# A fused attention and mixing kernel: other token tiles in the two rotation groups of the first batch

## The chip, the cores and the metric

One Trainium2 chip, one core. The metric is the device time of one execution in microseconds; lower is better. Three runs of the kernel before gave 989.75, 991.41 and 989.65 us, median 989.75.

## The reference, cut to what matters

Four batches, 8 heads, 576 tokens, 64 numbers per head (512 per token), in f32.

```
scores = q @ k^T / 8;  keep the 32 largest of each row;  attn = softmax;  x = attn @ v
theta  = x @ w_theta
zr, zi = x * cos(theta), x * sin(theta)
y      = w_tok_r @ zr + w_tok_i @ zi          # over the 576 tokens
u      = x + y;   x2 = u + relu(u @ w_ch)
h      = relu(x2 @ w_in);  u2, v2 = halves of h
out    = (u2 * (w_spatial @ layernorm(v2) + b_spatial)) @ w_out
```

The lines that matter here are the second to the fourth: the rotation (theta, cosine, sine and the two products) and the token mixing.

## The kernel before, in words

**Attention.** Work goes by tiles of 128 query rows; a batch has 4 pairs of heads with 9 tiles each, so 36 tiles, and two tiles make a group. For a group PE makes the scores (L449), ACT copies them to x (L453), and DVE finds the 32nd largest score of every row in a *round*: pairwise maxima and minima (L468, L469), maxima of eight (L472, L478), removals (L481), and the coefficients cf (L491). ACT then makes a sign and an exponential (L500, L501), POOL multiplies them (L89, written as sg), PE transposes (L511), ACT copies to ptb (L512), and PE multiplies by the values (L522 to L536). The result is normalised into xn. There are 72 rounds, on 144 tiles. x has three buffers, so fresh scores wait until POOL has done with those three groups earlier.

**The later layers** of batch b are run as a generator beside the attention of batch b + 1. Every product there is made of three matmuls on high and low parts (`mm3`, L572 to L574), since both operands are split in two. All instructions that a wrapper issues at raised priority carry L588. Parts of the generator of interest:

- `rotate(order)` works on the given token tiles (0 to 3 have 128 tokens, 4 the last 64). For every tile `theta` makes 12 matmuls, a rounding on ACT and DVE, and an absolute value on ACT. Then come the sines (cosines by a shifted bias) on ACT, for all tiles of the group together, in two halves of 256 columns. Then, for every quarter of 128 columns, DVE makes x * cos and x * sin, POOL copies the high part of the cosine product (zah) and DVE takes the low part (zal). In a second loop ACT copies the high part of the sine product (zbh) and POOL makes the low part (zbl). While they are angles, the same buffers appear in the trace as zbl and zbh; the sine product is written over xn.
- The last 64 tokens stand twice on the partitions, so that one sine with a bias of half a turn in one half gives both products; they form term 8.
- `middle(b)` begins with token mixing: 8 sums (4 blocks of 128 columns, 2 halves of 288 tokens) in PSUM, of 9 terms each: terms 0 to 3 are the cosine products of tiles 0 to 3, 4 to 7 the sine products, 8 the last tokens. A sum is added to F on DVE. Its PSUM tile, ps_m, has three buffers, shared with `theta`.

Batch 0 splits the rotation in two groups: `rotate((0, 1, 2))` is started when tile 36 is reached, before the last tiles of the batch are normalised, and `rotate((4, 3))` comes with the block of batch 0. The second group keeps its angles in two extra buffers (angle) and in r8. Token mixing of batch 0 takes the terms in another order than the other batches:

```python
terms = range(9) if b else (0, 1, 2, 4, 5, 6, 3, 7, 8)
```

so its first six terms need the first group alone. The other batches rotate all five tiles at once, in the order 0, 1, 4, 2, 3.

**What sets the order.** The generators yield costs, and `advance` lets them go on while the attention has given them credit. That and the priorities give the order of writing; a scheduler then lays down one list of instructions for every engine before the run. The split of the later weights into high and low parts (w_raw, w_f: L163 to L170, L211, L89, and SP's transfers) runs beside batch 0's attention and until round 26. The loads of the parts (L284) reuse the buffers of weights that are done with; `rotate` says so for w_theta when its group holds tile 4.

Of the kernel before, what the change touches and what calls it, by code (L numbers as in the profile page):

```python
# [10 lines left out]
F32 = mybir.dt.float32  # L11
F32R = mybir.dt.float32r
I32 = mybir.dt.int32
AF = mybir.ActivationFunctionType
OP = mybir.AluOpType
# [3 lines left out]
TURN = 6.283185  # L19
# [5 lines left out]
def sparse_attention_then_moe_kernel(  # L25
# [23 lines left out]
    NP = H // 2  # L49
# [19 lines left out]
    big = ctx.enter_context(tc.tile_pool(name="big", bufs=1))  # L69
# [37 lines left out]
    quarter, upright = constant(0.0, "quarter"), constant(math.pi / 2, "upright")  # L107
# [228 lines left out]
    def run(exact):  # L336
# [216 lines left out]

        XN = {}

        def normalise(b, j, lo, hi):
            if lo == 0:
                XN[b, j] = big.tile([128, 5, 2, D], F32, name="xn", bufs=6)
            xn = XN[b, j]
            i = slice(lo, hi)  # L560
            rs = tmp.tile([128, 5, 2], F32, name="rs")
            dve.tensor_scalar(rs[:, i], xr[:, i, :, D], 1e-9, None, op0=OP.add)
            dve.reciprocal(rs[:, i], rs[:, i])
            pool.tensor_tensor(xn[:, i], xr[:, i, :, 0:D], rs[:, i, :, None].to_broadcast([128, hi - lo, 2, D]),
                               op=OP.mult)
            if hi == 5:
                pool.tensor_tensor(xn[64:128, 4], xr[0:64, 4, :, 0:D],
                                   rs[0:64, 4, :, None].to_broadcast([64, 2, D]), op=OP.mult)


        def mm3(out, ah, al, bh, bl, first, last):
            pe.matmul(out, ah, bh, start=first, stop=False)  # L572
            pe.matmul(out, ah, bl, start=False, stop=False)  # L573
            pe.matmul(out, al, bh, start=False, stop=last)  # L574
# [82 lines left out]
        class Front:  # L657
# [59 lines left out]
            def rotate(self, order):  # L717

                ks = slice(min(order), min(max(order) + 1, 4))

                if order[0] == 0:
                    angles = zpair("b", F32)
                    rs, rc = (z[:, 0:2048].rearrange("p (k d) -> p k d", k=4)[:, ks] for z in angles)
                    r8 = angles[0][:, 2048:2560]
                else:
                    rs, rc = (big.tile([128, 1, 512], F32, name="angle", tag="xn", bufs=6) for _ in range(2))
                    r8 = t512()
                if self.b:
                    for i in order:
                        self.by_token(i, 0)  # L730
                    yield 2200
                for i in order:
                    if self.b == 0:
                        self.by_token(i, 0 if i == 4 else 3)
                    k = i - ks.start
                    ab = self.theta(i, *((r8, r8) if i == 4 else (rs[:, k], rc[:, k])))
                    yield 2600
                if 4 in order:
                    W.done(self.b, "th")

                with tc.issue_after(ab):
                    for d in (slice(0, 256), slice(256, 512)):
                        sin = uact.activation(rc[:, :, d], rc[:, :, d], AF.Sin, scale=-TURN, bias=upright)
                        uact.activation(rs[:, :, d], rs[:, :, d], AF.Sin, scale=-TURN)
                        if d.start == 0 and 4 in order:
                            with tc.issue_after(sin.ins):
                                uact.activation(r8, r8, AF.Sin, scale=-TURN, bias=quarter)
                zah, zal = self.za
                xs = [x_of(self.b, c) for c in range(4)]
                cols = [slice(c * 128, (c + 1) * 128) for c in range(4)]  # L750
                for x, d in zip(xs, cols):
                    udve.tensor_tensor(rc[:, :, d], x[:, ks], rc[:, :, d], op=OP.mult)
                    udve.tensor_tensor(x[:, ks], x[:, ks], rs[:, :, d], op=OP.mult)
                    if 4 in order:
                        udve.tensor_tensor(x[:, 4], x[:, 4], r8[:, d], op=OP.mult)
                    copy_pool(zah[:, ks, d], rc[:, :, d])
                    udve.tensor_tensor(zal[:, ks, d], rc[:, :, d], f32(zah[:, ks, d]), op=OP.subtract)
                    yield 1000
                if order[0] == 0:
                    self.zb = [z.rearrange("p (k d) -> p k d", k=5) for z in zpair("b")]  # L760
                zbh, zbl = self.zb
                ks = slice(ks.start, max(order) + 1)
                for i, (x, d) in enumerate(zip(xs, cols)):
                    copy_act(zbh[:, ks, d], x[:, ks])
                    self.turns[1 - i % 2].tensor_tensor(zbl[:, ks, d], x[:, ks], f32(zbh[:, ks, d]), op=OP.subtract)
                    yield 1000

        FR = {}

        def urgent(work):  # L770
            while True:
                with tc.high_priority(offset=FRONT):
                    c = next(work, None)
                if c is None:
                    return
                yield c
# [10 lines left out]
        def front(b):  # L787

            if b:
                FR[b] = Front(b)  # L790
                yield from FR[b].rotate((0, 1, 4, 2, 3))
            else:
                yield from urgent(FR[b].rotate((4, 3)))

        halves = [slice(0, HALF), slice(HALF, S)]

        def middle(b):
# [8 lines left out]
            for c in range(4):  # L806
                d = slice(c * 128, (c + 1) * 128)
                for m in halves:
                    p = mps([128, HALF])

                    terms = range(9) if b else (0, 1, 2, 4, 5, 6, 3, 7, 8)
                    for i, k in enumerate(terms):
                        mm3(p, *FR[b].z(k, d), th[k][:, m], tl[k][:, m], i == 0, i == 8)
                        if i == 5:
                            yield 1850
                    udve.tensor_tensor(F[:, c, m], p, F[:, c, m], op=OP.add)
                    lag.step(lambda c=c, m=m: ew.split(F[:, c, m], uh[:, c, m], ul[:, c, m]))
                    yield 1500
# [150 lines left out]
        def add_work(w):  # L969
            nonlocal work  # L970
            work = w if work is None else chain([work, w])
# [18 lines left out]
        def step(n):  # L990

            if n == RING:
                W.start()
            if n in EARLY:
                with tc.issue_after(FIRST[-1]):
                    early(EARLY.index(n))
            if n == PER:
                add_work(urgent(FR[0].rotate((0, 1, 2))))
            if n >= PER and (n - 4) % PER == 0:
                add_work(block(n // PER - 1))  # L1000
            if n < N:
                prepare(n)
# [90 lines left out]
```

## Time and profile before

| | |
|---|---|
| median of 3 runs | 989.75 us (989.65 to 991.41) |
| profiled execution | 992.02 us |
| its span, first to last instruction | 990.2 us |
| mean granted TensorE clock | 0.901 |
| PE, DVE, ACT, POOL busy | 867.8, 823.0, 638.0, 598.7 us |

The profile shows one execution. PE is TensorE's matmuls, DVE VectorE, ACT ScalarE, POOL GpSimd; SP issues the DMAs. A line of code can be that of a helper, so groups are told apart by the tiles: `out<-in`. Consecutive instructions of one engine overlap a little at their ends, so busy times of single rows add up to slightly more than the stretch that they fill.

### The profile page before, as it was taken

To read this page: it belongs to the slowest core of one execution; us is meant where nothing else is said; L and a number is where in the kernel's file an instruction comes from. 1 tells how busy PE (TensorE), PEld (TensorE's weight loads), DVE (VectorE), ACT (ScalarE), POOL (GpSimd) and SP (SyncE) were. 2 spreads that over 40 slices of the span, in tenths; PEclk is the share of its full clock that TensorE was granted. 3 is DMA by queue.
4 is the path that set the end of the run, shared out by engine and by line. 5 is a ranking of instruction groups with operands and counts; after the bars stand their busy time and mean duration, and the time that the engine had idled before them with its cause. 6 is when DMAs were issued, how large, how long until landed. Compare 5 with 4: busy or idle time off the path is not lost.

```text
span 990.2 us, 18081 instructions
## 1 busy us (share of the span) xinstructions
PE 867.8 (88%) x5802; PEld 797.5 (81%) x5802; DVE 823.0 (83%) x2710; ACT 638.0 (64%) x1319; POOL 598.7 (60%) x753
## 2 busy tenths in 40 slices
PE   4657686678779799989999999999989999999997
PEld 2546575667669798888889998898889998889987
DVE  6999999999998897889999998999998981363552
ACT  5566676779858566877776777777966775350121
POOL 2798876686956755594767666676584564421030
PEclk9955556679779699999999999899999999999999
DMA  7797665545817633744362753552743554441221
GB/s 218 215 305 227 215 210 179 145 145 186 261 60 199 230 95 106 229 143 126 110 206 60 229 160 78 218 129 95 205 160 91 201 188 166 191 168 62 104 85 52
DMA packets 79395, 159.78 MB, mean 161 GB/s; under 512 B 36143, under 2 KB 40239, under 8 KB 71866
## 3 DMA queue, kind: packets, MB, share of 16 engines
q1 hardware_dynamic: 79290, 158.53, 50.5%
q8 instruction: 48, 0.79, 0.3%
q14 instruction: 57, 0.47, 0.2%
HBM read 108.63 MB, written 23.32 MB: 133 GB/s over the span
## 4 chain that ended last, share of the span: by engine, by line
PE 43%; DVE 26%; ACT 10%; DMA 9%; POOL 6%; issue 4%; SPq 2%; ACTq 0%; POOLq 0%; DVEq 0%
PE ps_m L574 9%; PE ps_m L572 9%; PE ps_m L573 9%; PE ps_v L533 7%; DVE mm L469 4%; PE ps_s L449 4%; PE ps_t L511 4%; DVE mm L481 4%; DVE mx L478 4%; DVE z L472 2%; DVE mm L468 2%; DMA raw<-in_q_dram 2%; DMA q<-hi 2%; ACT sg L500 1%; POOL sg L89 1%
## 5 line engine op out<-in xcount | busy, mean ns | idle before, releaser
L89 POOL TENSOR_TENSOR sg<-x,sg 128x288 f32<-128x288 f32 x288 | 238.5, 857 | 141.0 <-ACT x L501 94.2
L511 PE MATMUL ps_t<-ident,sg 128*128 128x128 f32 x648 | 140.9, 314 | 60.7 <-POOL sg L89 37.5
L533 PE MATMUL ps_v<-vc,ptb 128*128 128x65 f32 (+1 forms) x1280 | 183.5, 281 | 4.7 <-ACT ptb L512 4.7
L533 PEld LDWEIGHTS ps_v<-vc,ptb 128*128 128x128 f32 (+1 forms) x1280 | 174.7, 206 | 13.6 <-ACT ptb L512 6.7
L511 PEld LDWEIGHTS ps_t<-ident,sg 128*128 128x128 f32 x648 | 97.8, 171 | 77.6 <-POOL sg L89 51.2
L500 ACT ACTIVATE sg<-x,cf 128x576 f32<-128x576 f32 x144 | 103.8, 768 | 44.2 <-DVE cf L491 43.3
L478 DVE MAX8 mx<-mm 128x8 f32<-128x160 f32 x432 | 118.8, 312 | 0.0
L453 ACT ACTIVATE x<-ps_s 128x576 f32<-128x576 f32 x144 | 92.6, 643 | 35.9 <-PE ps_s L449 32.3
L512 ACT ACTIVATE ptb<-ps_t 128x640 f32<-128x640 f32 (+1 forms) x144 | 92.7, 644 | 29.8 <-PE ps_t L511 28.2
L501 ACT ACTIVATE x<-x,cf 128x576 f32<-128x576 f32 x144 | 107.9, 767 | 0.1
L449 PE MATMUL ps_s<-k,q 128*128 128x288 f32 x256 | 91.3, 368 | 16.2 <-DVE q L369 8.6
L572 PE MATMUL ps_m<-w_t,zah 128*128 128x288 f32 (+2 forms) x272 | 98.9, 364 | 6.6 <-DVE F L588 4.8
L574 PE MATMUL ps_m<-w_t,zal 128*128 128x288 f32 (+2 forms) x272 | 97.5, 360 | 0.6 <-POOL zal L89 0.5
L573 PE MATMUL ps_m<-w_t,zah 128*128 128x288 f32 (+2 forms) x272 | 96.7, 356 | 0.0
L472 DVE MAX8 z<-mm 128x8 f32<-128x312 f32 (+1 forms) x288 | 89.6, 372 | 2.0
L572 PE MATMUL ps_m<-w_t,zbh 128*128 128x288 f32 x288 | 85.7, 302 | 2.3 <-DMA w_t<-d_sph 1.0
L481 DVE MATCH_REPLACE8 mm<-mx,mm 128x160 f32<-128x160 f32 x288 | 86.8, 308 | 0.0
L573 PE MATMUL ps_m<-w_t,zbh 128*128 128x288 f32 x288 | 86.2, 303 | 0.0
L574 PE MATMUL ps_m<-w_t,zbl 128*128 128x288 f32 x288 | 84.9, 302 | 1.2 <-POOL zbl L89 1.2
L449 PE MATMUL ps_s<-kl,q 128*128 128x288 f32 x256 | 82.9, 334 | 0.0
L468 DVE TENSOR_TENSOR mm<-x 128x576 f32<-128x576 f32 x72 | 67.7, 941 | 17.5 <-ACT x L453 16.4
L89 POOL TENSOR_TENSOR raw<-raw,hi 128x288 fp32r<-128x288 f32 x60 | 56.2, 956 | 40.2 <-ACT hi L393 40.0
(174 smaller groups left out, 2438.9 us busy)
## 6 DMA issues: line engine op xcount, KB each, us to landing
k<-hi SPq DMA_DIRECT2D x60, 144.0 KB, 2.5
kl<-raw SPq DMA_DIRECT2D x60, 144.0 KB, 2.6
vc<-in_v_dram SPq DMA_DIRECT2D x48, 128.0 KB, 2.9
w_t<-d_trh SPq DMA_DIRECT2D x4, 1152.0 KB
w_t<-d_trl SPq DMA_DIRECT2D x4, 1152.0 KB
out_dram<-t SPq DMA_DIRECT2D x32, 144.0 KB, 2.5
raw<-in_q_dram SPq DMA_DIRECT2D x15, 288.0 KB, 3.0
q<-hi SPq DMA_DIRECT2D x30, 144.0 KB, 3.3
```

The lines of the kernel that those rows point to most:

```text
L89: nc.gpsimd.tensor_tensor(out[:, lo:hi], a[:, lo:hi], b[:, lo:hi], op=op)
L449: pe.matmul(o, q, k[:, m], start=a == 0, stop=a == len(terms) - 1)
L472: dve.max(out=z[:, i, QUARTER + 8 * k:QUARTER + 8 * k + 8], in_=mm[:, i, losers])
L478: last = dve.max(out=top[i], in_=src[i])
L481: dve.match_replace(out=mr[i], in_to_replace=top[i], in_values=src[i], imm_value=NEG)
L500: act.activation(sg, x, AF.Sign, bias=cf[:, 2:3])
L501: act.activation(x, x, AF.Exp, bias=cf[:, 0:1], scale=0.125)
L511: pe.transpose(pt[:, c, :], x[:, lo:lo + 128], ident)
L533: pe.matmul(o, pt[:, c, q], chunks[:, c, slot], start=alone and c == 0, stop=not alone and i == 1 and c == 3)
L572: pe.matmul(out, ah, bh, start=first, stop=False)
L573: pe.matmul(out, ah, bl, start=False, stop=False)
L574: pe.matmul(out, al, bh, start=False, stop=last)
```

## The change

Batch 0's first group gets tile 3, and the second keeps the last tokens alone. Since tile 3 of the last head pair may not have been normalised when the first group is started, the generator yields until it is (`WHOLE`). The last tokens' sine is issued by itself; the second group needs no angle buffers, no cosine and no low parts of it. Within each quarter the last tokens' product comes ahead of the others. Token mixing takes its terms in order in every batch, and the pause inside a sum is behind the fifth term instead of the sixth.

```diff
+        WHOLE = set()
...
             if hi == 5:
+                if j == NP - 1:
+                    WHOLE.add(b)
...
                 else:
-                    rs, rc = (big.tile([128, 1, 512], F32, name="angle", tag="xn", bufs=6) for _ in range(2))
                     r8 = t512()
...
                 for i in order:
+                    while i > 2 and self.b not in WHOLE:
+                        yield 600
...
                 with tc.issue_after(ab):
-                    for d in (slice(0, 256), slice(256, 512)):
+                    if order == (4,):
+                        uact.activation(r8, r8, AF.Sin, scale=-TURN, bias=quarter)
+                    for d in (slice(0, 256), slice(256, 512)) if order[0] == 0 else ():
...
                 for x, d in zip(xs, cols):
+                    if 4 in order:
+                        udve.tensor_tensor(x[:, 4], x[:, 4], r8[:, d], op=OP.mult)
+                    if order == (4,):
+                        continue
                     udve.tensor_tensor(rc[:, :, d], x[:, ks], rc[:, :, d], op=OP.mult)
                     udve.tensor_tensor(x[:, ks], x[:, ks], rs[:, :, d], op=OP.mult)
-                    if 4 in order:
-                        udve.tensor_tensor(x[:, 4], x[:, 4], r8[:, d], op=OP.mult)
...
-                yield from urgent(FR[b].rotate((4, 3)))
+                yield from urgent(FR[b].rotate((4,)))
...
-                    terms = range(9) if b else (0, 1, 2, 4, 5, 6, 3, 7, 8)
-                    for i, k in enumerate(terms):
-                        mm3(p, *FR[b].z(k, d), th[k][:, m], tl[k][:, m], i == 0, i == 8)
-                        if i == 5:
+                    for k in range(9):
+                        mm3(p, *FR[b].z(k, d), th[k][:, m], tl[k][:, m], k == 0, k == 8)
+                        if k == 4:
                             yield 1850
...
-                add_work(urgent(FR[0].rotate((0, 1, 2))))
+                add_work(urgent(FR[0].rotate((0, 1, 2, 3))))
```

The lists of instructions show what moves. DVE in the kernel before, from the start of round 22 (L588 are the rotation's instructions; zbl and zbh hold the angles, xn the attention output):

```order
L468 TENSOR_TENSOR mm<-x 128x2x288
L469 TENSOR_TENSOR mm<-x 128x2x288
L485 TENSOR_TENSOR flags<-z,mx 128x4
L588 TENSOR_TENSOR zbl<-xn,zbl 128x3x128 x4
L468 TENSOR_TENSOR z<-mm 128x2x144
L588 TENSOR_TENSOR xn<-xn,zbh 128x384 x4
L469 TENSOR_TENSOR mm<-mm 128x2x144
L588 TENSOR_TENSOR zal<-zbl,zah 128x3x128
L491 SCALAR_TENSOR_TENSOR cf<-cf,mx 128x2
L588 TENSOR_TENSOR zal<-zbl,zah 128x3x128
L588 COPY F<-ps_m 128x128
L588 TENSOR_TENSOR zal<-zbl,zah 128x3x128 x2
```

DVE in the changed kernel, from the start of round 23 (its L592 is the line that was L588); round 22 holds no product of the rotation there:

```order
L468 TENSOR_TENSOR mm<-x 128x2x288
L469 TENSOR_TENSOR mm<-x 128x2x288
L468 TENSOR_TENSOR z<-mm 128x2x144
L592 TENSOR_TENSOR zbl<-xn,zbl 128x4x128 x2
L469 TENSOR_TENSOR mm<-mm 128x2x144
L592 TENSOR_TENSOR zbl<-xn,zbl 128x4x128 x2
L592 TENSOR_TENSOR xn<-xn,zbh 128x512 x2
L472 MAX z<-mm 128x8 x4
L592 TENSOR_TENSOR xn<-xn,zbh 128x512
L592 TENSOR_TENSOR zal<-zbl,zah 128x4x128
L491 SCALAR_TENSOR_TENSOR cf<-cf,mx 128x2
L592 TENSOR_TENSOR xn<-xn,zbh 128x512
```

The rotation of tiles 0 to 3 stands one round later and in wider instructions, and the coefficients cf of round 23 stand behind eight of them.

SP's DMA issues in the kernel before, around the loads of w_tok_i's parts (d_tih, d_til); sp is w_spatial, w_f the buffers of the conversion:

```order
L199 DMA w_f<-in_moe_w_spatial_dram 128x576
L284 DMA w_t<-d_tih 128x2304
L409 DMA kl_2663<-raw 64x576 x2
L224 DMA d_sph<-w_f 128x576
L409 DMA kl_2664<-raw 64x576
L225 DMA d_spl<-w_f 128x576
L284 DMA w_t<-d_til 128x2304
```

and in the changed kernel:

```order
L225 DMA d_spl<-w_f 128x576
L409 DMA kl_2653<-raw 64x576
L408 DMA k_2651<-hi 64x576
L409 DMA kl_2653<-raw 64x576
L199 DMA w_f<-in_moe_w_spatial_dram 64x576
L224 DMA d_sph<-w_f 128x576
L199 DMA w_f<-in_moe_b_spatial_dram 1x576
L387 DMA raw<-in_q_dram 128x576
L225 DMA d_spl<-w_f 128x576
L284 DMA w_t<-d_tih 128x2304
L284 DMA w_t<-d_til 128x2304
```

Both loads have moved behind one more part of w_spatial and now stand next to each other.

## Rows read from the trace of the kernel before

**Rows 1.** The span in 40 slices, busy tenths of PE and DVE (page).

```profile
PE   4657686678779799989999999999989999999997
DVE  6999999999998897889999998999998981363552
```

**Rows 2.** Windows at rounds 22 to 25: busy us, instructions; clock, DMA share, GB/s.

```profile
246.30:266.60 20.30, 16.54 (x76) 13.87 (x76) 20.27 (x47) 16.68 (x32) 18.50 (x24) 0.72 0.77 242
266.60:282.20 15.60, 12.80 (x96) 11.82 (x95) 15.57 (x48) 13.26 (x26) 13.40 (x19) 1.00 0.51 163
282.20:299.50 17.30, 11.82 (x71) 11.59 (x70) 14.72 (x42) 8.29 (x18) 8.24 (x11) 0.70 0.19 59
299.50:314.80 15.30, 15.30 (x115) 13.95 (x114) 12.70 (x41) 11.50 (x22) 8.54 (x10) 1.00 0.79 217
```

**Rows 3.** DVE's groups by shape, 236 to 300 us: busy us, mean ns | idle before.

```profile
L588 DVE TENSOR_TENSOR xn<-xn,zbh 128x384 f32<-128x384 f32 x4 | 3.8, 1001 | 0.0
...
L588 DVE TENSOR_TENSOR zbl<-xn,zbl 128x384 f32<-128x384 f32 x4 | 3.3, 894 | 0.0
L588 DVE TENSOR_TENSOR zal<-zbl,zah 128x384 fp32r<-128x384 f32 x4 | 3.0, 762 | 0.0
L588 DVE TENSOR_TENSOR zal<-angle,zah 128x128 fp32r<-128x128 f32 x4 | 2.8, 768 | 0.0
...
L588 DVE TENSOR_TENSOR angle<-xn,angle 128x128 f32<-128x128 f32 x4 | 1.6, 456 | 0.0
...
L588 DVE TENSOR_TENSOR xn<-xn,angle 128x128 f32<-128x128 f32 x4 | 1.1, 326 | 0.0
...
L588 DVE SCALAR_TENSOR_TENSOR zbh<-t,ps_m 128x512 f32<-128x512 f32 x1 | 0.7, 650 | 0.0
```

**Rows 4.** DVE in order of time: start us, duration us, [idle before, releaser].

```profile
269.24 0.75 DVE L491 SCALAR_TENSOR_TENSOR cf<-cf,mx 128x2 f32<-128x2 f32 x1
...
282.18 2.93 DVE L468 TENSOR_TENSOR mm<-x 128x576 f32<-128x576 f32 x1
...
299.03 0.46 DVE L588 TENSOR_TENSOR F<-ps_m,F 128x288 f32<-128x288 f32 x1 [2.51 <-PE ps_m L574]
...
305.64 0.96 DVE L163 TENSOR_SCALAR w_f<-w_raw 128x512 int32<-128x512 int32 x1 [2.54 <-POOL sg L89]
...
324.55 1.42 DVE L468 TENSOR_TENSOR mm<-x 128x576 f32<-128x576 f32 x1
...
338.66 1.06 DVE L468 TENSOR_TENSOR mm<-x 128x576 f32<-128x576 f32 x1 [3.48 <-ACT x L453]
```

**Rows 5.** ACT in order of time, rounds 23 and 24.

```profile
267.15 1.28 ACT L588 ACT_TABLE_LOAD   x1
...
286.48 1.44 ACT L500 ACTIVATE sg<-x,cf 128x576 f32<-128x576 f32 x2 [3.86 <-DVE cf L491]
```

**Rows 6.** SP in order of time: the loads of w_tok_i's two parts.

```profile
254.12 0.33 SPq L284 DMA_DIRECT2D w_t<-d_tih  x1
...
262.43 0.33 SPq L284 DMA_DIRECT2D w_t<-d_til  x1
```

**Rows 7.** PE in order of time: token mixing (ps_m) and scores (ps_s) of rounds 22 to 27.

```profile
259.47 0.58 PE L572 MATMUL ps_m<-w_t,zah 128*128 128x288 f32 x1 [3.50 <-DVE F L588]
...
264.41 0.42 PE L574 MATMUL ps_m<-w_t,zal 128*128 128x288 f32 x1
...
266.01 0.51 PE L572 MATMUL ps_m<-w_t,zbh 128*128 128x288 f32 x2
...
266.50 0.29 PE L573 MATMUL ps_m<-w_t,zah 128*128 128x288 f32 x1
...
288.56 1.11 PE L511 MATMUL ps_t<-ident,sg 128*128 128x128 f32 x4 [5.48 <-ACT ptb L512]
...
295.21 0.39 PE L449 MATMUL ps_s<-k,q 128*128 128x288 f32 x1
...
324.15 0.29 PE L574 MATMUL ps_m<-w_t,zbl 128*128 128x288 f32 x1
```

## The prediction

> **What bounds the kernel now.** I read the slices of the span first. From the second slice DVE stands at 8 or 9 tenths, once at 7, up to slice 33, and at 1 to 6 behind it, while PE, at 4 to 8 in the first twelve, goes on at 9 almost to the end [rows 1]. So there are two regimes: up to the last of the 72 top-k rounds DVE sets the pace, and behind it PE works off the last batch alone. A microsecond that DVE saves before the last round moves the rest of the program forward, as long as PE and the buffers follow.
>
> I count a round from the first pairwise maximum on fresh scores (L468 with x as its input) to the next one. Batch 0's rotation lies in rounds 22 and 23, its token mixing in rounds 22 to 27. Next come the windows cut at these rounds [rows 2]: in round 22 (20.3 us) DVE is busy 20.27, in round 23 (15.6 us) 15.57, and PE has 16.54 and 12.80 there. In round 24 (17.3 us) DVE has 14.72 and PE 11.82: both wait. In round 25 PE is full.
>
> The order of instructions is laid down before the run, and between the two kernels it differs only in this stretch: from round 42 on each of the four compute engines and SP has the same list in both, row for row, to the end of the first run. What the change is worth is decided between rounds 21 and 41 and kept afterwards.
>
> **Part 1, DVE: 24 instructions become 12.** The first group's cosine product, sine product and cosine low part are three times four instructions of 128x384 [rows 3]: 3.3 + 3.8 + 3.0 = 10.1 us. The second group's are three times four of 128x128: 1.6 + 1.1 + 2.8 = 5.5 us. Together 15.6 us on a full DVE. Twelve of 128x512 replace them, all in round 23; the four products of the last tokens stay.
>
> No row has this operation at 512 columns. Lower end: a DVE instruction of 128x512 that reads one operand from PSUM has a mean of 0.65 us [rows 3], so 12 x 0.65 = 7.8. Upper end: the 384-column forms cost 10.1 / 12 = 0.84 each, and in proportion 512 columns would cost 1.12, so 13.4. I take the line through the two groups: 5.5 / 12 = 0.46 for 128 columns and 0.84 for 384 give 0.19 per 128 more, so 1.03 for 512, and 12 x 1.03 = 12.4. These are the nearest rows, because POOL works beside both kernels' rotation: in round 22 it is busy 18.50 of 20.3 us [rows 2]. **Gain 15.6 - 12.4 = 3.2 us**, between 2.2 and 7.8.
>
> **Part 2, the fourth sum of token mixing.** In round 24 DVE takes four sums from PSUM, and before the fourth it sits idle 2.51 us, until 299.03, for PE [rows 4]. Round 25 stands behind it in DVE's queue. In the new list that fourth addition stands in round 25, behind its pairwise instructions, so round 25 no longer waits for it. **Gain 2.5 us**; 0 if PE is as late for the third sum, which still stands in round 24.
>
> **What I cost at nothing.** The five theta products keep their number; tile 3's comes before that of the last tokens instead of after. ACT has nine sine instructions now and five then, with the same columns, and two table loads for sine and two back either way, 1.28 us each [rows 5]; ACT was busy 16.68 of 20.3 us in round 22 [rows 2], and that slack covers it; without it the first product would wait for the sines. POOL's high copies go from eight to four with the same columns; its sine low parts stay twelve, eight of 256 columns and four of 128. The moved pause inside a sum (behind the fifth term instead of the sixth) and the terms in order leave the 216 matmuls of the token mixing as they were.
>
> SP's queue is one that work is moved past. The loads of w_tok_i's two parts were issued at 254.12 and 262.43 [rows 6]; the first was used at 266.01 [rows 7], so it took at most 11.9 us. Now both stand behind a part of w_spatial that POOL has to finish first. I put both at the later of the two times, so they are there by 274 at the latest. Their first user comes behind the first sums' 24 cosine matmuls, at 272 or so (next part): at most 2 us of PE's time, which the margin there covers. Without it PE would be late by as much as the loads are.
>
> **Part 3, PE starts later.** The first token-mixing matmul was at 259.47, behind round 22's low parts [rows 7]. Round 22 without its rotation is 20.3 - 10.1 = 10.2 us, so round 23 starts at about 256.5; before the first low part lie that round's four pairwise instructions and four maxima (some 3.5 us, by the other rounds) and seven products of 1.03 us: PE starts at about 267, 7.7 later. PE has to be through three sums before the scores of tile 49, which are now issued behind them: 72 matmuls at 0.13 to 0.24 us are 9.5 to 17 us, so 277 to 284, and the last tokens' terms come at about 281. Before, these scores were at 295.21 [rows 7]. Besides, PE stood idle for 5.48 us until 288.56, and that takes up most of the later start. So I cost it at nothing: round 25 has some 10 us in hand for its x.
>
> PE restarted at 259.47 after 3.50 us of waiting; at 264.41 a matmul still took 0.42 us, at 266.50 it took 0.29 [rows 7]: these are the two levels, 1.2 and 2.4 GHz, 0.24 and 0.13 us from one to the next. The Trainium skill ("TensorE: Matmul & The Clock Gate", Part 1) says that an idle TensorE falls to the lower clock and has to be busy for a while to get the full one back. The trace agrees, by those three rows. By that rule a longer idle stretch ahead of token mixing makes its first matmuls slow, which speaks against this change; the price is in the second rival.
>
> **Sum.** -3.2 - 2.5 = -5.7 us. The profiled execution took 992.02 us (span 990.2), 2.27 above the median of 989.75; against it 986.3, and against the median **984.0**. The ends of parts 1 and 2 give gains of 2.2 to 10.3, so 979.5 to 987.6 for this case alone.
>
> **The rivals.**
> *More is gained.* Two further losses of the stretch may go. Round 25 loses 2.54 us in front of a weight conversion [rows 4], which has to wait until an earlier one has left its buffer; in the new list conversions begin in round 23. And round 24's first instruction took 2.93 us against 1.42 in round 27 [rows 4]; both stood beside POOL, and POOL's work moves against DVE's. For it: the conversions come a round earlier. Against it: DVE and POOL meet somewhere else. 5.7 + 2.5 + 1.5 = 9.7 us: 980.0. Chance 0.20.
> *PE becomes the bound (slower).* From 288.56 to the end of token mixing at 324.15 PE has hardly room [rows 2, 7]. It starts 7.7 us later; if all 72 matmuls run at the lower level, instead of the some 20 from 259.47 to 264.41, 52 x 0.11 = 5.7 us come on top. The idle 5.5 us takes part of it, and 3.5 us hide in DVE's wait for x in front of round 28 [rows 4]: 7.7 + 5.7 - 5.5 - 3.5 = +4.4 us, and what DVE saves is lost in waiting for PE: 994.1. It decides once the scores of tile 49 come later than 295.2. For it: the late loads and the clock. Against it: I have those scores 10 us earlier. Chance 0.15.
> *Saved and lost again (no change).* The coefficients cf for the weighting came 2.6 us into round 23 (269.24, [rows 4]); now seven products and a low part precede them, so they come some 12 us in. Signs, exponentials, POOL's products, transposes and the release of x hang on them; ACT waited 3.86 us for them in round 24 [rows 5]. If round 25 then waits 4 to 6 us for x, the gain is gone: 989.7. Chance 0.13.
> That the change does not happen is excluded by the list: it has the twelve wide instructions.
>
> **How the numbers follow.** The main case has 0.52 and gives 984.0. A measurement of this kernel tells about 0.2%, 2 us, from no change. Faster by more: main case and first rival, 0.72; the same 0.13; slower 0.15. The range reaches from a little under the first rival, 978.5, to a little over no change, 990.5; it leaves out the slower rival and the far end of the first, about 0.2.
>
> **What would show it.** Round 22 about 10 us and round 23 about 23; twelve 128x512 instructions at about 1.03 us; no wait of 2.5 us for PE in front of an F addition in round 24; scores of tile 49 at 282 to 287; round 26 at about 309 instead of 314.8, and the shift the same at the last round. The prediction is wrong if the twelve take over 1.3 us each, if DVE waits for x or for a sum in rounds 24 to 28 by more than before, or if the shift at round 26 is lost by round 42.

## The result, and the profile after

| | before | after |
|---|---|---|
| median, us | 989.7 (987.24 to 991.41, 4 runs) | 979.07 (976.44 to 980.63, 4 runs) |
| profiled execution: time, span | 992.02, 990.2 | 980.12, 978.2 |
| mean granted clock of TensorE | 0.901 | 0.926 |

The ratio is 0.9891, with a 95% interval of 0.9869 to 0.9913: 10.6 us faster by the medians, where 5.7 were forecast. 979.07 lies just inside the range, at its fast end.

**Where the time went.** Stages are cut at the starts of the rounds (first pairwise maximum, L468, with x as its input), in the two profiled executions:

| us | before | after | difference |
|---|---|---|---|
| up to round 22 | 246.33 | 245.71 | -0.62 |
| rounds 22 and 23 | 35.85 | 32.78 | **-3.07** |
| rounds 24 and 25 | 32.63 | 32.63 | 0.00 |
| rounds 26 and 27 | 23.85 | 19.23 | **-4.62** |
| rounds 28 to 37 | 107.67 | 102.50 | **-5.17** |
| round 38 to the start of round 72 | 352.50 | 354.02 | +1.52 |
| start of round 72 to the end | 191.37 | 191.33 | -0.04 |

The profiled execution of before was 2.3 us above the median of its kernel and that of after 1.05, so some 1.4 us of these 12.0 come from the choice of executions.

The slices of the page, PE and DVE, after; beside [rows 1] the two regimes are the same:

```profile
PE   3748576679679999999999999899989999999997
DVE  6999999999998998999899998999998971463552
```

The windows of rounds 22 to 25, to be read beside [rows 2], then rounds 26 and 27 (columns: window, length, busy PE, PEld, DVE, ACT, POOL with their instructions, clock, DMA share, GB/s):

```profile
245.71:256.33 10.62, 8.37 (x35) 7.72 (x36) 10.51 (x34) 8.29 (x17) 7.91 (x10) 0.57 0.84 259
256.33:278.49 22.16, 16.87 (x98) 15.13 (x97) 20.07 (x45) 17.64 (x27) 18.14 (x21) 0.82 0.67 225
278.49:295.85 17.36, 10.98 (x58) 9.53 (x57) 16.64 (x44) 11.17 (x21) 14.28 (x18) 0.71 0.24 73
295.85:311.12 15.27, 15.27 (x129) 14.70 (x127) 12.73 (x41) 12.29 (x27) 8.00 (x10) 1.00 0.61 189
311.12:319.40 8.28, 8.28 (x65) 8.28 (x65) 8.21 (x36) 7.63 (x21) 4.74 (x8) 1.00 0.42 118
319.40:330.35 10.95, 9.41 (x78) 9.11 (x76) 10.85 (x33) 6.99 (x14) 10.79 (x14) 1.00 0.94 343
```

Rounds 22 and 23 are as forecast, 10.6 and 22.2 us. In round 24 DVE waits less than before but is busy 16.64 us instead of 14.71, and the round is no shorter.

DVE's groups by shape in rounds 23 and 24 of after (busy us, mean ns | idle before), beside [rows 3]:

```profile
L592 DVE TENSOR_TENSOR xn<-xn,zbh 128x512 f32<-128x512 f32 x4 | 3.7, 938 | 0.0
L592 DVE TENSOR_TENSOR xn<-xn,t 128x128 f32<-128x128 f32 x4 | 3.3, 879 | 0.0
L592 DVE TENSOR_TENSOR zal<-zbl,zah 128x512 fp32r<-128x512 f32 x4 | 3.2, 826 | 0.0
L592 DVE TENSOR_TENSOR zbl<-xn,zbl 128x512 f32<-128x512 f32 x4 | 3.0, 786 | 2.1 <-ACT zbl L592 2.1
```

The twelve wide instructions take 3.7 + 3.2 + 3.0 = 9.9 us in place of 15.6, but the first of them waits 2.1 us for the cosines, and the four products of the last tokens (second row) take 3.3 us.

DVE of after in order of time, the rows that answer to [rows 4]:

```profile
261.35 1.29 DVE L592 TENSOR_TENSOR zbl<-xn,zbl 128x512 f32<-128x512 f32 x2 [2.09 <-ACT zbl L592]
...
270.15 0.75 DVE L491 SCALAR_TENSOR_TENSOR cf<-cf,mx 128x2 f32<-128x2 f32 x1
...
278.49 0.75 DVE L468 TENSOR_TENSOR mm<-x 128x576 f32<-128x576 f32 x1
...
280.37 1.29 DVE L164 SCALAR_TENSOR_TENSOR w_f<-w_raw,w_f 128x512 int32<-128x512 int32 x1
281.58 3.28 DVE L592 TENSOR_TENSOR xn<-xn,t 128x128 f32<-128x128 f32 x4
...
292.37 0.46 DVE L592 TENSOR_TENSOR F<-ps_m,F 128x288 f32<-128x288 f32 x1 [0.66 <-PE ps_m L578]
...
304.66 0.97 DVE L163 TENSOR_SCALAR w_f<-w_raw 128x512 int32<-128x512 int32 x1 [1.70 <-ACT w_f L211]
...
330.35 0.74 DVE L468 TENSOR_TENSOR mm<-x 128x576 f32<-128x576 f32 x1
```

The 2.51 us in front of round 24's last F sum (the fourth before, the third after, as the fourth now stands in round 25) have become 0.66, round 24's first instruction takes 0.75 instead of 2.93, the 2.54 in front of a weight conversion 1.70, and the 3.48 us for x in front of round 28 are gone.

PE of after in order of time, beside [rows 7]:

```profile
263.18 0.40 PE L576 MATMUL ps_m<-w_t,zah 128*128 128x288 f32 x1 [2.76 <-POOL zah L592]
...
271.16 0.29 PE L578 MATMUL ps_m<-w_t,zal 128*128 128x288 f32 x1
...
290.76 0.61 PE L449 MATMUL ps_s<-k,q 128*128 128x288 f32 x1 [3.64 <-ACT x L453]
...
292.13 0.44 PE L576 MATMUL ps_m<-w_t,zah 128*128 128x288 f32 x1
...
324.48 0.29 PE L578 MATMUL ps_m<-w_t,zbl 128*128 128x288 f32 x1
```

And SP, beside [rows 6]; the prediction put both loads at 262.43:

```profile
261.89 0.38 SPq L284 DMA_DIRECT2D w_t<-d_tih  x1
262.32 0.47 SPq L284 DMA_DIRECT2D w_t<-d_til  x1
```

**Busy or waiting.** The window from round 22 to round 38, before and then after:

```profile
246.33:446.33 200.00, 176.80 (x1199) 163.18 (x1198) 176.96 (x593) 141.27 (x301) 140.55 (x173) 0.90 0.54 167
```

```profile
245.71:432.85 187.14, 168.02 (x1191) 157.11 (x1191) 175.93 (x581) 140.02 (x295) 139.25 (x167) 0.93 0.57 176
```

DVE is busy 176.96 and 175.93 us there, hardly less; its idle time falls from 23.0 to 11.2. So in sum 11.8 of the 12.9 us gained in this stretch are waits that are gone. The instruction time saved in rounds 22 and 23 came back elsewhere: DVE is busy 1.9 us longer in round 24, and 96.92 us instead of 93.47 in rounds 28 to 37, where it does nearly the same work (355 and 358 instructions) and its idle time falls from 14.2 to 5.6 us. POOL is busy there for 75.38 us instead of 69.98; whether that is the reason no run shows. The waits that DVE had in the same stretch, first before, then after (us in total, times, longest):

```profile
DVE mm L468 <- ACT x L453: 7.3, 4, 3.5
DVE st L588 <- ACT t L588: 5.7, 3, 3.5
DVE w_f L163 <- POOL sg L89: 2.5, 1, 2.5
DVE F L588 <- PE ps_m L574: 2.5, 1, 2.5
```

```profile
DVE st L592 <- ACT t L592: 2.4, 3, 1.0
DVE zbl L592 <- ACT zbl L592: 2.1, 1, 2.1
DVE w_f L163 <- ACT w_f L211: 1.7, 1, 1.7
```

The largest entry of before, DVE waiting for fresh scores in x, is not among the first of after. That wait was in no term of the main case.

**Round 27.** In PE's list of before, tile 55's scores stand behind the transposes and the values of tile 49; in that of after they stand ahead of tile 49's transposes. Round 28 needs the scores of tiles 54 and 55. PE of before, from the transposes of tile 49:

```profile
333.69 1.11 PE L511 MATMUL ps_t<-ident,sg 128*128 128x128 f32 x4 [2.13 <-ACT ptb L512]
...
336.59 0.59 PE L449 MATMUL ps_s<-k,q 128*128 128x288 f32 x1
```

ACT copied them to x at 338.00, behind two signs and two exponentials of the next tiles, and DVE began round 28 at 338.66. In after tile 55's scores begin at 326.31 and round 28 at 330.35. Why the two lists differ there is only argued: token mixing starts later, so that in after PE still has its matmuls until 324.8, well into round 27, where before they had run out at 324.4, as the round began.

### The profile page after: what moved, and what is told of

It is laid out like the page before. It is cut to its first block, busy times and chain, and to the rows that moved or that the text cites. A ratio compares the mean times of both kernels' runs of the same rounds, so it can differ in the third digit from the quotient of the medians.

```text
span 978.2 us, 18058 instructions
## 1 busy us (share of the span) xinstructions
PE 852.8 (87%) x5802; PEld 784.8 (80%) x5802; DVE 822.4 (84%) x2698; ACT 636.1 (65%) x1315; POOL 597.0 (61%) x749
## 4 chain that ended last, share of the span: by engine, by line
PE 43%; DVE 28%; ACT 9%; DMA 8%; POOL 7%; issue 4%; SPq 2%; POOLq 0%; ACTq 0%; DVEq 0%
PE ps_m L578 9%; PE ps_m L576 9%; PE ps_m L577 9%; PE ps_v L533 6%; DVE mm L469 4%; DVE mx L478 4%; DVE mm L481 4%; PE ps_s L449 4%; PE ps_t L511 3%; DVE z L472 3%; DVE mm L468 3%; POOL sg L89 2%; DMA q<-hi 2%; POOL zbl L89 2%; ACT sg L500 1%
## 5 line engine op out<-in xcount | busy, mean ns | idle before, releaser
L533 PE MATMUL ps_v<-vc,ptb 128*128 128x65 f32 (+1 forms) x1280 | 179.2, 278 | 4.4 <-ACT ptb L512 4.4
L511 PE MATMUL ps_t<-ident,sg 128*128 128x128 f32 x648 | 137.4, 307 | 50.4 <-POOL sg L89 35.1
L533 PEld LDWEIGHTS ps_v<-vc,ptb 128*128 128x128 f32 (+1 forms) x1280 | 170.4, 202 | 13.2 <-ACT ptb L512 6.8
L576 PE MATMUL ps_m<-w_t,zah 128*128 128x288 f32 (+2 forms) x272 | 97.7, 359 | 5.7 <-POOL zah L592 2.8
L577 PE MATMUL ps_m<-w_t,zah 128*128 128x288 f32 (+2 forms) x272 | 95.7, 352 | 0.0
L449 PEld LDWEIGHTS ps_s<-k,q 128*128 128x128 f32 x256 | 56.3, 220 | 29.9 <-ACT x L453 20.8
```

What stands on the lines that cost most here:

```text
L449: pe.matmul(o, q, k[:, m], start=a == 0, stop=a == len(terms) - 1)
L511: pe.transpose(pt[:, c, :], x[:, lo:lo + 128], ident)
L533: pe.matmul(o, pt[:, c, q], chunks[:, c, slot], start=alone and c == 0, stop=not alone and i == 1 and c == 3)
```

## The experiments

"Shift" is the start of a round in the kernel less that in the profiled execution of before; the stretch behind the last round is counted from the start of round 72. The theories: the **saved work** of the rotation carries the gain and all behind it follows; or the **order** of PE and ACT behind round 25, which came out differently, carries most of it. After the first runs a third question arose: what becomes of a gain behind round 38. The three comparisons stood beside medians of before of 990.64, 988.37 and 989.64 us.

### Parts of the change

**regroup_only**, the change without its token-mixing part:

```
-                    for k in range(9):
+                    terms = range(9) if b else (0, 1, 2, 4, 5, 6, 3, 7, 8)
+                    for i, k in enumerate(terms):
...
-                        if k == 4:
+                        if i == 5:
```

> The changed kernel, but token mixing takes its nine terms in the old order with the old pause. Order theory: the regrouping alone sets how the instructions stand on PE and ACT; tile 55's scores still come ahead of tile 49's transposes, so rounds 22 and 23 together last about 33 us, round 27 about 11 us with no wait for x before round 28, and the time is 979 to 983. Theory that the terms in order bring what comes behind round 25: round 27 stays near 14 us with the 3.5 us wait for x, and the time is 986 to 988 (only the 3.1 us of rounds 22 and 23).

Measured: 986.9 us, ratio 0.9954 (0.9935 to 0.9973). Rounds 22 and 23 took 33.79, rounds 26 and 27 18.74, and no wait for x stood before round 28: so far the order theory. The time is that of the other theory. At round 38 the shift was still -12.0, at round 72 -15.9; but the stretch behind the last round took 201.68 us instead of 191.33. The pause went back together with the terms, and no run parts them.

**terms_only**, the kernel before with

```
-                    terms = range(9) if b else (0, 1, 2, 4, 5, 6, 3, 7, 8)
+                    terms = range(9)
```

> The kernel before, with its groups (0,1,2) and (4,3), but token mixing takes its terms in order. Order theory: nothing is saved in rounds 22 and 23 (35.9 us together), tile 55's scores stand behind tile 49's transposes as in the kernel before, round 27 keeps a wait for x of 2 to 4 us, and the time is 988 to 991. Theory that the terms in order bring the gain behind round 25: round 27 falls to 11 us and the time to 981 to 984.

Measured: 990.53, ratio 1.0002 (0.9981 to 1.0023). Rounds 26 and 27 took 25.10; the wait in round 27 was not for x but 3.3 us for an F sum. In the total the order of the terms by itself gains nothing. But at round 72 its shift was -12.0, that of the change, without one instruction saved; it was lost behind the last round, which took 200.12 us.

**pace_1300**, the kernel before, its rotation handed out at another pace:

```
-                    yield 1000
+                    yield 1000 if self.b else 1300
```

> The kernel before with no instruction added or taken away: only the pace at which batch 0's rotation is handed out (1300 for 1000 in each step) differs, and with it the order in which instructions stand between rounds 21 and 49; tile 55's scores come ahead of tile 49's transposes. Order theory: the 3.48 us wait for x in front of round 28 shrinks to under 1 us, and the time is 984 to 988. Theory that the gain is saved DVE work: 24 instructions of rotation as before, so 989 to 991.

Measured: 985.51, ratio 0.9943 (0.9915 to 0.9972): 5 us faster with the same instructions. The wait before round 28 was gone and rounds 26 and 27 took 19.43, though 2.25 us of waiting for x then stood before round 29. Rounds 22 to 25 took 65.54 us with all 24 instructions, 65.41 in the change with 12. Order alone can bring half of what the change brought.

**narrow**, the change with each wide instruction in two:

```
-                    udve.tensor_tensor(rc[:, :, d], x[:, ks], rc[:, :, d], op=OP.mult)
...
+                    parts = (ks,) if self.b else (slice(0, 3), slice(3, 4))
+                    for t in parts:
+                        udve.tensor_tensor(rc[:, t, d], x[:, t], rc[:, t, d], op=OP.mult)
...
```

> The changed kernel, but each of the twelve 128x512 instructions of the rotation is split again into 128x384 and 128x128. Theory that the gain is the saved DVE work and everything behind it merely follows: 3.1 us are lost and the rest kept, 981 to 984. Order theory: besides those 3.1 us the order falls back (tile 55's scores behind tile 49's transposes), round 27 is 13 to 14 us again with a wait for x, and the time is 986 to 991.

Measured: 988.93, ratio 0.9978 (0.9960 to 0.9996), with a wait of 2.04 us for x before round 28 and rounds 26 and 27 at 22.25. The number is the order theory's, and rounds 26 and 27 fell back as it said. But at round 72 the shift was -12.5, no less than that of the change; the total was lost behind the last round, in 202.21 us, as in regroup_only.

### Round 27, and other paces

PE runs at its lower clock in round 27 of before (0.56, and 0.76 in round 28), in after at 1.00. So the clock could be the cause rather than the order. **fill_18** and **fill_24** keep PE busy where it stood idle, with 18 or 24 matmuls whose sum nobody reads:

```
+            if b == 0:
+                p = mps([128, HALF])
+                for k in range(18):
+                    pe.matmul(p, FR[0].z(k % 9, d)[0], th[k % 9][:, m], start=k == 0, stop=k == 18 - 1)
             for n in ("tr", "ti", "t9"):
```

> The kernel before plus 18 matmuls of 128x288 whose sum nobody reads, in PE's list between the last matmul of token mixing and the transposes of tile 48, where PE stood idle in round 27; up to the transposes of tile 50 every other instruction keeps its place. Theory that the lower clock and the idle PE of rounds 27 and 28 cost the time: the granted clock of rounds 26 to 28 is 0.95 or more instead of 0.80, and round 28 starts 2.5 to 5 us earlier than 338.66 although work was added. Theory that it was ACT's order alone (the copy of x behind the signs and exponentials): the 3.48 us wait for x in front of round 28 stays at 2.5 us or more and round 28 starts within 1 us of 338.66. The total says less, since behind round 28 the order differs and 20 more matmuls stand behind the last round (3 us): 985 to 990 by the first, 991 to 995 by the second.

> The same with 24 matmuls; with them tile 55's scores come to stand ahead of tile 49's transposes. Theory of clock and order together: no wait for x before round 28, which starts 5 us or more earlier than 338.66, and with 18 matmuls fewer behind the last round than the kernel before the time is 980 to 985, faster than the kernel before with 24 matmuls more. Theory that the gain is the saved DVE work of the rotation: nothing is saved here, 990 to 993.

Measured: fill_18 996.75, ratio 1.0072 (1.0044 to 1.0099); fill_24 993.75, ratio 1.0054 (1.0029 to 1.0078). Both totals missed. Round 27 decides what they were made for. The windows of round 27, then PE and DVE in order of time; first fill_18:

```profile
322.88:336.99 14.11, 9.60 (x52) 8.39 (x51) 10.81 (x34) 8.61 (x17) 11.44 (x14) 0.77 0.97 370
```

```profile
332.05 1.12 PE L511 MATMUL ps_t<-ident,sg 128*128 128x128 f32 x4 [2.34 <-ACT ptb L512]
...
334.96 0.59 PE L449 MATMUL ps_s<-k,q 128*128 128x288 f32 x1
```

```profile
336.99 0.76 DVE L468 TENSOR_TENSOR mm<-x 128x576 f32<-128x576 f32 x1 [2.77 <-ACT x L453]
```

Now fill_24, where tile 55's scores come first:

```profile
319.76:330.24 10.48, 6.41 (x31) 5.14 (x30) 9.85 (x32) 6.48 (x13) 9.86 (x12) 0.73 0.99 353
```

```profile
328.19 0.61 PE L449 MATMUL ps_s<-k,q 128*128 128x288 f32 x1 [1.38 <-ACT x L453]
...
329.32 1.06 PE L511 MATMUL ps_t<-ident,sg 128*128 128x128 f32 x4
```

```profile
330.24 0.78 DVE L468 TENSOR_TENSOR mm<-x 128x576 f32<-128x576 f32 x1 [0.56 <-ACT x L453]
```

fill_18 raised the clock from 0.56 to 0.77 and gained nothing: round 27 took 14.11 us, as before. fill_24 had 0.73, its scores ran at the lower level (0.24 us from one matmul to the next), and round 27 took 10.48. But fill_18's clock over rounds 26 to 28 was 0.86, not the 0.95 of the expectation. Two runs from above close this gap. The windows of round 27, first narrow (scores behind), then pace_1300 (ahead):

```profile
317.92:331.21 13.29, 11.17 (x92) 10.73 (x90) 10.71 (x33) 8.59 (x20) 10.81 (x13) 1.00 0.98 296
```

```profile
319.32:329.22 9.90, 5.86 (x27) 4.90 (x27) 9.80 (x33) 7.14 (x14) 9.90 (x12) 0.54 1.01 399
```

At a clock of 1.00 the round is long with the scores behind, and at 0.54 it is short with them ahead. The clock is not the cause; the place of tile 55's scores goes with the gain.

**after_pace_700** and **after_pace_1300**, the change with the edit of pace_1300 (and 700), were meant to shorten the stretch behind the last round.

> The changed kernel with batch 0's rotation handed out at a pace of 700 for 1000; work and instructions are the same, the order differs from tile 52 on, and 26 matmuls fewer stand behind the last round. Theory that PE's order behind round 26 sets the time: the tail behind the last round is 187 to 188 us instead of 191.3, and the time 974 to 978. Theory that the DVE work of the rotation sets it: 978 to 980 as for the change.

> The changed kernel with a pace of 1300 for 1000: same work, the order differs from round 22 on, and again 26 matmuls fewer stand behind the last round. Theory that PE's order behind round 26 sets the time: a tail of 187 to 188 us and 973 to 979. Theory that the DVE work of the rotation sets it: 978 to 980.

Measured: 990.09, ratio 1.0002 (0.9976 to 1.0029), and 992.4, ratio 1.0033 (1.0000 to 1.0067). The stretch behind the last round was shortened as expected, to 187.84 and 187.67. But the gain of -14.3 us at round 38 of after_pace_700 was lost by round 72 (+3.6): between them 370.41 us, against 354.02. Their order differs from that of before to the end, while that of the change is the same as before's from round 42 on.

### Orders that come back

So pairs were looked for in which the order does come back. **narrow_return** is narrow at a pace of 1300, **regroup_return** is regroup_only at 1600, **before_return** the kernel before with another pace in token mixing:

```
-                    yield 1500
+                    yield 1500 if b else 1600
```

> The changed kernel with its twelve 128x512 instructions split again into 128x384 and 128x128 (24, as before), at a rotation pace of 1300, with which the order comes back to that of the changed kernel by round 33 and stays there. Theory that the saved DVE instructions count in full at the end: 2 to 5 us slower than the changed kernel in the same comparison, 981 to 985. Theory that order is all, and the DVE time is swallowed by PE behind round 26: within 1.5 us of the changed kernel, 978 to 981.

> The kernel of the run regroup_only (new groups, terms in the old order) at a rotation pace of 1600, with which the order comes back to that of both kernels by round 45. Theory that the later loss of regroup_only came from an order that never came back, and not from the terms: the shift at the last round is within 2 us of that at round 45, the tail 191 to 192 us, and the time 977 to 982. Theory that the terms in order are worth 6 to 8 us by themselves: 985 to 988.

> The kernel before, with 1600 for 1500 as the pace of token mixing's second halves: no instruction added or taken away, tile 55's scores still behind tile 49's transposes, the same order up to round 28 and again from round 49 on. Theory that the loss of the kernel before sits in the order of rounds 27 and 28: the wait for x before round 28 stays at 2.5 us or more, and of the gain of the change little comes: 985 to 990. Theory that any other order of rounds 28 to 42 gains what the change gained there: 980 to 985.

> The changed kernel itself, to stand beside the other three on the same chip: 977 to 981 by every theory, rounds 22 and 23 together 32 to 34 us, no wait for x of over 1 us between rounds 26 and 37, a tail of 191 to 192 us.

Measured in one comparison: change_again 979.21, ratio 0.9896 (0.9855 to 0.9936); narrow_return 985.22, ratio 0.9942 (0.9917 to 0.9967); regroup_return 988.18, ratio 0.9973 (0.9947 to 0.9999); before_return 988.25, ratio 0.9981 (0.9957 to 1.0005).

- narrow_return is 6.0 us slower than the change beside it. It took 68.78 us in rounds 22 to 25, against 65.40 in change_again, and 105.64 in rounds 28 to 37, against 103.26. So the forecast of the theory that order is all, within 1.5 us, failed. But the 3.4 us cannot be read as the price of the instructions. The 24 took 14.5 us and the twelve 10.5 (durations added up), yet DVE as a whole is busy for 60.64 and 60.28 us in these rounds; what differs is its idle time, 8.1 and 5.1 us (windows below the list). The pace too changes the list there: the orders differ up to round 32. At the same pace of 1300 the twelve instructions of after_pace_1300 took 65.00 us in these rounds; at the pace of 1000 the 24 of narrow took 64.81, less than the change. What the saved instructions are worth at the end is therefore not shown, nor where the 2.4 us further on come from.
- regroup_return kept its shift from round 45 (-3.1) to round 72 (-3.4) and had its tail of 191.89. But it lost 10 us in rounds 38 to 44, before the order had come back. So the loss without the new order of the terms came twice, at two places, and both times behind round 37. That the terms cost nothing where they stand is shown (rounds 22 to 28); that a third order could keep the gain without them was not tried.
- before_return kept its 3.48 us wait and its rounds 26 and 27 at 23.13. It gained 4.2 us in rounds 28 to 37, without any saved instruction, and gave back 3.5 by round 72.

The windows of rounds 22 to 25, narrow_return and then change_again:

```profile
246.50:315.28 68.78, 52.15 (x318) 47.67 (x319) 60.64 (x171) 48.51 (x92) 48.63 (x57) 0.80 0.54 168
```

```profile
244.37:309.77 65.40, 51.74 (x313) 47.71 (x313) 60.28 (x159) 49.08 (x91) 48.34 (x57) 0.79 0.55 178
```

All profiled executions, one of each kernel, in us. That of fill_24 was 6.0 us and that of after_pace_1300 3.5 us below its kernel's median, the others within 2.9 us of it. The last column is the round from which the order is that of before (a dash: never).

| kernel | tile 55's scores | rounds 22-25 | 26, 27 | 28-37 | 38 to end | order back by round |
|---|---|---|---|---|---|---|
| before | behind | 68.48 | 23.85 | 107.67 | 543.87 | |
| before_return | behind | 68.62 | 23.13 | 103.44 | 547.86 | 49 |
| fill_18 | behind | 67.80 | 23.83 | 105.52 | 553.29 | - |
| terms_only | behind | 62.78 | 25.10 | 99.76 | 551.62 | - |
| narrow | behind | 64.81 | 22.25 | 106.55 | 550.74 | - |
| fill_24 | ahead | 64.30 | 20.20 | 103.63 | 552.03 | - |
| pace_1300 | ahead | 65.54 | 19.43 | 107.35 | 545.43 | 49 |
| after | ahead | 65.41 | 19.23 | 102.50 | 545.35 | 42 |
| change_again | ahead | 65.40 | 19.11 | 103.26 | 545.56 | 42 |
| narrow_return | ahead | 68.78 | 18.71 | 105.64 | 544.67 | 42 (that of the change by 33) |
| regroup_only | ahead | 66.31 | 18.74 | 104.39 | 550.23 | - |
| regroup_return | ahead | 64.86 | 18.44 | 103.10 | 553.79 | 45 |
| after_pace_700 | ahead | 65.50 | 18.53 | 101.57 | 558.25 | - |
| after_pace_1300 | ahead | 65.00 | 18.86 | 105.81 | 551.92 | - |

Two columns divide without overlap: rounds 26 and 27 take 22.3 to 25.1 us with tile 55's scores behind tile 49's transposes and 18.4 to 20.2 ahead of them; and from round 38 to the end the kernels whose order never came back take 550.2 to 558.3, the others 543.9 to 547.9, but for regroup_return. In terms_only the long round 27 goes with the wait for an F sum, so the place of the scores is not the whole mechanism. No kernel that was run is faster than the change.

## Why the prediction was right, and where it was not

That 979.07 fell inside the range was in good part luck: of the 12.0 us between the two profiled executions 3.1 came where the sum had a term for them and 9.8 in rounds that were set to no change, while 1.5 were given back behind them.

**Part 1 held, by two errors that cancel.** Forecast 3.2 us; 3.07 measured in rounds 22 and 23 (3.67 in change_again, against the same before). The twelve took 0.83 us each, not 1.03: the line through the 128- and 384-column forms was too steep, and 9.9 us were nearer the lower bound of 7.8. That alone gives 5.7; DVE's busy time in the two rounds fell by 5.3, from 35.84 [rows 2] to 30.58. Against it stand 2.09 us of waiting for the cosines (0.97 in change_again), costed at nothing because of ACT's slack in round 22; that slack did not cover it, and the sentence that named the wait as what would come without cover was right. That these microseconds reach the end is not shown: pace_1300 has none of the saving and gains as much in rounds 22 to 25.

**Part 2 failed.** The wait for the fourth F sum shrank by 1.85 us, but rounds 24 and 25 were not shorter: the four products of the last tokens, moved to where POOL is at work, took 3.28 us instead of 0.88. "The four products of the last tokens stay" was the step that failed; their number stayed, not their price. And the wait was no fixed loss: with the same order up to there the kernels before, before_return and fill_18 waited 2.5, 2.5 and 2.0 us for a sum in rounds 22 to 25, fill_24 not at all, its clock in round 24 being 1.00 instead of 0.70.

**Part 3 held in its result.** Token mixing began at 263.18 and in earnest at 271.16, forecast 267. The scores of tile 49 came at 290.76, later than the 282 to 287 forecast because they waited 3.64 us for ACT, but still before 295.2. The slow rival, the clock at its lower level through all of token mixing, did not come: from 271.16 to 281 the matmuls stand 0.13 us apart. But the lower level came back once: from 284.46 to 294.77, around waits of 0.59, 0.90 and 3.64 us, those that follow each other directly stand 0.24 us apart, and then 0.13 again. The late cf of the third rival came (270.15, 13.8 us into round 23), and no wait for x followed in round 25.

**What was missed** is the step "what the change is worth is decided between rounds 21 and 41 and kept afterwards": it held here to within 1.8 us, but only Parts 1 and 2 were priced, both before round 26. The order was known to differ up to round 41, and everything behind round 26 was set to no change. It brought 9.8 us: 4.6 with tile 55's scores, and 5.2 in rounds 28 to 37, whose cause no run isolates. The wait of 3.48 us for x stood in the rows and was used only as cover in the slow rival; it should have been a term.

**The number of the first rival, not its mechanism.** "More is gained" gave 980.0. Of its two losses round 24's first instruction did fall, by 2.2 us, and the conversion's wait by 0.8, and both were used up in the same two rounds, which stayed at 32.63.

**"The shift the same at the last round" held only from round 38 on**: -13.5 there, -12.0 at round 72. That it held at all goes with the order being that of before again from round 42 on, which the prediction read off the lists and which seven of the experiments lacked.

## What to carry to other kernels

Where a scheduler lays down the order, cost an edit in two parts: what it removes, and every stretch in which its list differs from the old one; look there for an instruction that the next round waits for and see whether it stands ahead of or behind a transfer of other work. Find the row from which the lists are the same again: here a gain made before it was kept to within some 2 us, and a list that never came back could lose more than the edit saved. To price one part by undoing it, a variant whose order comes back is not enough; the list up to there must be the same as well. narrow was 0.2% faster than before where the change was 1.1% faster, and narrow_return 6.0 us slower than the change, and neither figure is the price of the twelve instructions.

## What the runs showed that was not expected

**The same list, with the clock falling or not.** From round 42 on before and after have the same order; yet round 64 took 10.67 us in one and 12.20 in the other. The windows, before and after:

```profile
725.41:736.08 10.67, 8.08 (x61) 7.38 (x60) 10.57 (x35) 5.90 (x12) 10.03 (x13) 1.00 0.39 160
```

```profile
711.88:724.08 12.20, 9.68 (x61) 8.93 (x61) 10.26 (x35) 5.92 (x12) 10.03 (x13) 0.86 0.35 143
```

In both PE had waited three times for POOL, 1.74, 0.54 and 0.31 us before, 1.67, 0.54 and 0.32 after. PE then, before and after:

```profile
731.61 0.29 PE L573 MATMUL ps_m<-w_t,zbh 128*128 128x288 f32 x1
731.74 0.29 PE L574 MATMUL ps_m<-w_t,zbl 128*128 128x288 f32 x1
```

```profile
718.49 0.44 PE L576 MATMUL ps_m<-w_t,zbh 128*128 128x288 f32 x1
718.73 0.44 PE L577 MATMUL ps_m<-w_t,zbh 128*128 128x288 f32 x1
```

The matmuls stand 0.13 us apart in one and 0.24 in the other, the levels of 2.4 and 1.2 GHz, and DVE then waits for two F sums. Of seven profiled executions with this list three kept the clock (10.67 to 10.68 us) and four did not (12.15 to 12.82). This is the 1.5 us that the change gives back. The change has two of these executions, both with 12.20 us, the other kernels one each; whether chance decides or the kernel is not shown. The Trainium skill ("TensorE: Matmul & The Clock Gate", Part 1) says that the stretches over which the chip judges activity run freely and do not begin with the program, so that the point of the change varies. The trace agrees: nearly the same gaps, two outcomes.

**The same four products at 0.88 and at 3.28 us.** Before they stood at 273.25, while POOL was idle (from 272.8 to 274.7); after they stand at 281.58, beside POOL's products. Before (DVE, then POOL), and then POOL of after:

```profile
273.25 0.88 DVE L588 TENSOR_TENSOR xn<-xn,t 128x128 f32<-128x128 f32 x4
274.68 3.23 POOL L89 TENSOR_TENSOR sg<-x,sg 128x288 f32<-128x288 f32 x4 [1.89 <-ACT x L501]
```

```profile
279.79 4.13 POOL L89 TENSOR_TENSOR sg<-x,sg 128x288 f32<-128x288 f32 x4
```

The Trainium skill ("SBUF — State Buffer", Who interferes with whom) says that a VectorE instruction with two inputs in SBUF and a GpSimd instruction that reads SBUF block each other for a whole instruction. The trace agrees: 0.22 us each alone, 0.82 each beside POOL.
